# Attention's first batch ends in three steps, its first expert weights arrive earlier

## The chip, the cores and the metric

The kernel runs on one core of a Trainium2 chip. The metric is the device time of one execution, in microseconds (us). TensorE is PE in the profile, VectorE is DVE, ScalarE is ACT, GpSimd is POOL; SyncE (SP) issues every DMA of this kernel, in order.

## The reference

Three parts, each feeding the next.

```
scores = scale * q @ k^T            # 2 batches, 8 heads, 576 positions, head width 64, float32
scores = where(mask, scores, -1e9)  # heads 0-3: the last 32 positions; heads 4-7: every 32nd position
attn   = softmax(scores);  x = attn @ v                 # x: 1152 tokens x 512
p      = domain_probs / sum(domain_probs)               # 4 experts
x      = sum_e p[:, e] * (relu(x @ w1[e]) @ w2[e])      # w1: 512 x 1024, w2: 1024 x 512
out    = (sigmoid(x @ w_gate) * (x @ w_val)) @ w_out    # 512 x 1536, 1536 x 512
```

## The kernel before, in words

Attention comes first, batch by batch. One batch is 16 groups: 8 "s" groups (strided heads 4 to 7, in residues of 8 positions) and 8 "l" groups (local heads 0 to 3). Groups 0 to 15 belong to batch 0, groups 16 to 31 to batch 1. A group passes through stages, one per step of the generator `attention`: scores (PE, two groups at a time, output `sps`), exp (DVE takes the negated row maximum `nm`, ACT the exponentials `P` with their sums `sm`), norm one step later (DVE reciprocal of `sm`, POOL scales `P`), transpose three steps later (PE to `tps`, DVE copies it to `PT`), values (PE to a PSUM tile `o`, for every second group) and split. The split writes x as two parts, `xh` rounded and `xl` the remainder, into tiles of 384 tokens (T = 0, 1, 2): batch 0 fills tile 0 and half of tile 1. For a local group of the second half this is 96 tokens of tile 0 and 192 of tile 1.

The products are made from such pairs: `split_products` issues three matmuls per product (high by high, low by high, high by low). The weights come as float32 `raw` tiles of 512 KB each; `prep_early` turns one into `wh` (an ACT cast) and `wl` (a POOL subtraction), two `early_step` calls for each of its 128-row blocks. Three raw tiles fit at once. `early_up` (four blocks fb of 12 matmuls) and `early_down` are the first expert's units; ACT evacuates an `early_up` block to `hh`, DVE its remainder to `hl`, and DVE evacuates an `early_down` block into `x2acc`, multiplied by `p` (tile `p00`), the token weights. These are computed on DVE from `ptok` (`token_weights`), transposed on PE (`pps`), copied to `ptokT`, written to DRAM (`pd`) and read back spread over all partitions (`p`) by `spread_token_weights`.

The order of the work is the order in which the program is written out: every engine takes its instructions in that order. `attend()` emits one step of attention and, by the step's number, some loads. The first `FIRST_GROUPS` steps are emitted alone (with `early_step` calls between); from then on a step is emitted after every 1 / 0.36 products of the early units. `EMPTY` gives the steps in which PE gets matmuls on zeros (`warm`). `head_start(fb)` issues the first half of block fb of the first `early_up` (the weight rows 2 and 3, which need only the strided heads) ahead of the rest of attention; its PSUM bank stays taken until that block is done.

Eight PSUM banks are in use: the pool `gp` (tag g) has four, `sps` three, the pool `ops` one. All of the transposes, the head starts, the early units' outputs and some `o` tiles take turns in the four banks of `gp`; a new tile waits until all readers of the tile that had the bank before are done. The second strided q and k of batch 1 are in the tile `qk`; `qk_strided` transposes q on PE into `qkps` (ACT copies it to `qsT`), then k (DVE copies it to `ksT`); `qk_local` does the same for the local q and k in three parts.

The three lines on which most depends:

```
gp = ctx.enter_context(tc.tile_pool(name="gp", bufs=PSUM_BUFS, space=PSUM))      # PSUM_BUFS = 4
step_of = [x + DRAIN * (x // (n // B)) for x in range(n)]                        # DRAIN steps between the batches
dve.tensor_tensor(a, ps, pb[e, T], ALU.mult)                                     # early_down's first evacuation, pb is p
```

Of the kernel before, what the change touches and what calls it, by code (L numbers as in the profile page):

```python
# [35 lines left out]
EMPTY = {0: 2, 1: 4, 2: 2, 3: 2, 4: 2, **{i: 2 for i in range(5, 16, 2)}, 16: 1, 19: 1, 20: 1}  # L36
# [11 lines left out]
FIRST_GROUPS = 21  # L48
PT_BUFS = 5
WEIGHTS_FROM = 12  # L50
DRAIN = 5
HEAD_START = (17, 18)
# [54 lines left out]
def attn_moe_glu_kernel(ctx, tc, q, k, v, dp, w1, w2, wg, wv, wo, out):  # L107
# [12 lines left out]
    NU = S // 8  # L120
# [641 lines left out]
    def group_values(g):  # L762
# [20 lines left out]
        if at_step[0] in range(WEIGHTS_FROM, FIRST_GROUPS):  # L783
            of_tiles[g] = o, o
            return
# [4 lines left out]
    def group_split(g):  # L790

        kind, b, c, half, hh = g
        if hh == 0:
            return
        o, of = of_tiles.pop(g)
        low = dve if of is o else pool_
        if kind == "s":
            kk = 2 + c
            hv, ov = (t[:, :288].rearrange("p (a u) -> p a u", u=NU) for t in (o, of))
            for T, off, s0, n in x_parts(b, 0, S):  # L800
                u0, u1 = s0 // 8, (s0 + n) // 8
                sel = lambda t: t[T][:, kk, off:off + n].rearrange("p (u a z) -> p z a u", a=4, z=2)[:, half]
                dve.tensor_copy(sel(xh), hv[:, :, u0:u1])
                low.tensor_tensor(sel(xl), ov[:, :, u0:u1], sel(xh).bitcast(F32), ALU.subtract)
        else:
            for T, off, s0, n in x_parts(b, 288 * half, 288 * half + 288):
                p0 = s0 - 288 * half
                dh, dl = xh[T][:, c, off:off + n], xl[T][:, c, off:off + n]
                dve.tensor_copy(dh, o[:, p0:p0 + n])
                low.tensor_tensor(dl, of[:, p0:p0 + n], dh.bitcast(F32), ALU.subtract)  # L810
# [3 lines left out]
    def attention():  # L814
# [13 lines left out]
        at_stage = {}  # L828
        for name, behind in STAGES:
            for x in range(n):  # L830
                if name in ("values", "split"):
                    if x % QUAD >= 2:
                        at_stage[name, step_of[x] + behind + later(x)] = gs[x]
                elif name == "scores":
                    if x % 2 == 0:
                        at_stage[name, step_of[x]] = gs[x:x + 2]
                else:
                    at_stage[name, step_of[x] + behind] = gs[x]
        qk_strided(0, 0, (0,))
        for i in range(step_of[-1] + STAGES[-1][1] + 1):  # L840
            at_step[0] = i
            for name, _ in STAGES:
                if (name, i) in at_stage:
                    stage[name](at_stage[name, i])
            if i == 0:
                qk_strided(0, 0, (1,))
            if i in HEAD_START:
                head_start(HEAD_START.index(i))
            if i in EMPTY:
                keep_warm(EMPTY[i])  # L850
            for b in range(B):
                at = i - step_of[b * n // B]
                if b and at in (-5, -3):
                    qk_strided(b, 0, (int(at == -3),))
# [388 lines left out]
    with tc.manual_schedule():  # L1243
# [3 lines left out]
        make_constants()  # L1247
        load_local(0)
# [7 lines left out]
        def attend():  # L1256
# [23 lines left out]
        for i in range(FIRST_GROUPS):  # L1280
            attend()
            for _ in range((i >= WEIGHTS_FROM) + (i > 15)):
                early_step(0)
        n_none, n_step = 0, [0]
# [22 lines left out]
        for n, u in enumerate(units):  # L1307
# [33 lines left out]
            for y in unit_steps(u):  # L1341
                if n < N_EARLY:
                    if y is None:
# [45 lines left out]
```

## Time and profile before

| | us |
|---|---|
| median of 3 runs (650.66 to 651.46) | 650.7 |
| the profiled execution | 651.06 |
| its span, first to last instruction | 648.9 |
| PE busy in the span | 638.2 (98%) |
| DVE, ACT, POOL busy | 440.3, 341.7, 265.5 |

The span is 2.2 us shorter than the execution's own time, which also has what lies before the first and after the last instruction. PE's granted clock is full in all 40 slices of the page. A row of the timeline gives the start in the span, the length, the engine, the line in the kernel, the operation with output and inputs, and in brackets how long the engine had been idle and what ended that. Matmul rows overlap, since matmuls are pipelined, so the distance between two starts is what one costs. One transpose, score or value product of float32 can show as two matmuls. Some matmul rows can be missing.

### The profile page before, as it was taken

Reading aid. Unit: us, or ns where it says so; the run is one execution under the profiler, and the core shown is the slowest. Engines: PE = TensorE matmul, PEld = TensorE weight load, DVE = VectorE, ACT = ScalarE, POOL = GpSimd, SP = SyncE. Lnnn points to the kernel's source line nnn. Section 1 sums busy time; section 2 is a strip of 40 time slices with the busy share of each in tenths; the row PEclk is TensorE's granted clock in tenths of the full one; section 3 lists DMA queues with packets and bytes.
Section 4 is the critical chain, followed back from the end, with each engine's and each line's share of the span. In section 5 each row is a group of like instructions: output and inputs, shape, how many; then the busy total and the mean of one; then the engine's idle time right before and its main releaser. Section 6 shows DMA issues by size and latency. Waiting matters only on the chain.

```text
span 648.9 us, 12702 instructions
## 1 busy us (share of the span) xinstructions
PE 638.2 (98%) x4899; PEld 469.3 (72%) x4904; DVE 440.3 (68%) x885; ACT 341.7 (53%) x807; POOL 265.5 (41%) x307
## 2 busy tenths in 40 slices
PE   8889999999999999999999999999999999999998
PEld 5668889999676666666666666666979877987794
DVE  4876586787461886693887788898866659633432
ACT  5747553554854646774645554642565574532230
POOL 3665561000422226361335335440465377453540
PEclk9999999999999999999999999999999999999999
DMA  9965141030421544251664464354113832330002
GB/s 184 243 172 141 35 117 43 1 115 17 142 86 57 158 147 159 81 182 59 183 255 143 163 227 147 98 162 146 35 34 117 286 142 81 107 132 1 33 19 97
DMA packets 48884, 77.00 MB, mean 119 GB/s; under 512 B 19540, under 2 KB 24440, under 8 KB 47672
## 3 DMA queue, kind: packets, MB, share of 16 engines
q1 hardware_dynamic: 48824, 76.20, 37.6%
q8 instruction: 38, 0.62, 0.4%
q14 instruction: 22, 0.18, 0.1%
HBM read 59.66 MB, written 16.53 MB: 117 GB/s over the span
## 4 chain that ended last, share of the span: by engine, by line
PE 94%; DVE 1%; DMA 1%; SPq 1%; ACT 1%; issue 0%; POOL 0%; POOLq 0%; ACTq 0%
PE gps L874 23%; PE gps L876 23%; PE gps L875 23%; PE gps L976 19%; SPq L173 1%; PE sps L730 1%; PE warm L264 1%; PE tps L756 1%; PE o L780 1%; DMA ks<-in_k_dram 1%; ACT P L101 1%; DMA kl<-in_k_dram 1%; PE qkps L698 0%; PE qkps L676 0%; PE sps L717 0%; DVE nm L101 0%
## 5 line engine op out<-in xcount | busy, mean ns | idle before, releaser
L101 POOL TENSOR_TENSOR hl<-t,hh 128x384 f16<-128x384 f32 x72 | 76.5, 1065 | 179.2 <-ACT t L101 175.4
L976 PEld LDWEIGHTS <-w 128*128 128x128 f16 x1512 | 125.0, 98 | 1.8
L976 PE MATMUL gps<-x,w 128*128 128x192 f16 x1512 | 126.2, 246 | 0.0
L874 PE MATMUL gps<-x,w 128*128 128x384 f16 x288 | 93.9, 326 | 0.0
L875 PE MATMUL gps<-x,w 128*128 128x384 f16 x288 | 93.9, 326 | 0.0
L876 PE MATMUL gps<-x,w 128*128 128x384 f16 x288 | 93.9, 326 | 0.0
L874 PE MATMUL gps<-hh,w 128*128 128x384 f16 x288 | 93.9, 326 | 0.0
L875 PE MATMUL gps<-hl,w 128*128 128x384 f16 x288 | 93.9, 326 | 0.0
L876 PE MATMUL gps<-hh,w 128*128 128x384 f16 x288 | 93.9, 326 | 0.0
L874 PEld LDWEIGHTS <-w 128*128 128x128 f16 x576 | 56.4, 98 | 37.3 <-issue 0.2
L876 PEld LDWEIGHTS <-w 128*128 128x128 f16 x576 | 56.4, 98 | 37.2
L875 PEld LDWEIGHTS <-w 128*128 128x128 f16 x576 | 56.4, 98 | 36.4
L101 ACT ACTIVATE hh<-gps 128x384 f16<-128x384 f32 (+1 forms) x96 | 46.8, 487 | 48.8 <-PE gps L876 48.5
L101 POOL TENSOR_TENSOR stage<-magn,stage 128x512 f16<-128x512 f32 x36 | 45.5, 1273 | 45.1 <-ACT magn L101 38.9
L101 ACT ACTIVATE w<-raw,up 128x512 f16<-128x512 f32 x48 | 32.0, 715 | 34.8 <-DVE up L101 34.7
L101 ACT ACTIVATE P<-sps,nm 72x72 f32<-72x72 f32 (+1 forms) x112 | 36.4, 333 | 23.8 <-DVE sm L101 17.0
L101 ACT ACTIVATE bits<-raw 128x512 f32<-128x512 f32 x36 | 24.3, 674 | 38.1 <-DVE magn L101 37.9
L101 DVE SCALAR_TENSOR_TENSOR w<-raw,up,w 128x512 f16<-128x512 f32 x48 | 40.1, 871 | 5.1 <-ACT w L101 4.9
L101 POOL TENSOR_TENSOR sg<-four,sg 128x384 f32<-128x384 f32 x9 | 9.6, 1069 | 80.8 <-DVE four L101 77.9
L874 PE MATMUL gps<-w,hh 128*128 128x512 f16 (+1 forms) x112 | 41.6, 371 | 0.0
L875 PE MATMUL gps<-w,hh 128*128 128x512 f16 (+1 forms) x112 | 41.6, 371 | 0.0
L876 PE MATMUL gps<-w,hl 128*128 128x512 f16 (+1 forms) x112 | 41.6, 371 | 0.0
(145 smaller groups left out, 1281.5 us busy)
## 6 DMA issues: line engine op xcount, KB each, us to landing
raw<-in_moe_w_dram SPq DMA_DIRECT2D x32, 512.0 KB
raw<-in_moe_w_gate_dram SPq DMA_DIRECT2D x12, 512.0 KB
raw<-in_moe_w_val_dram SPq DMA_DIRECT2D x12, 512.0 KB
raw<-in_moe_w_out_dram SPq DMA_DIRECT2D x12, 512.0 KB
wg<-stage SPq DMA_DIRECT2D x21, 256.0 KB
wv<-stage SPq DMA_DIRECT2D x21, 256.0 KB
w<-wg SPq DMA_DIRECT2D x3, 1024.0 KB
wo<-stage SPq DMA_DIRECT2D x12, 256.0 KB
```

The costliest lines, as they stand in the source:

```text
L101: return f(*a, **k)
L173: nc.sync.dma_start(t[:, :, j, :], src[b, 2 * j:2 * j + 2].rearrange("h s d -> (h s) d").rearrange("(c p) d -> p c d", p=128),)
L264: nc.tensor.matmul(ps, zero.to_broadcast([128, 128]), zero.to_broadcast([128, 512]), start=True, stop=True,)
L730: nc.tensor.matmul(pv_[:, j, :], qs_, ks_, start=False, stop=j == m - 1)
L756: nc.tensor.transpose(pv_[:, j, :], pp[:, j, :], ident[:n, :n])
L780: nc.tensor.matmul(o[x * 64:x * 64 + 64, j * n:(j + 1) * n], lhsT, tts[x][:, j, :], start=True, stop=True)
L874: nc.tensor.matmul(ps, ah, bh, start=first and i == 0, stop=False)
L875: nc.tensor.matmul(ps, ah, bl, start=False, stop=False)
L876: nc.tensor.matmul(ps, al, bh, start=False, stop=last and i == n - 1)
L976: nc.tensor.matmul(o, l_, r_, start=first and x + kk + y == 0, stop=last and x * kk * y == 2, skip_group_check=True)
```

## The change

It does six things together.

- The last steps of batch 0 shrink from five (16 to 20) to three (16 to 18): eight entries of the stage table are moved. The values and split of group 11 go from step 17 to 16, the transposes of 14 and 15 from 17 and 18 to 16 and 17, the values of 14 and 15 from 19 and 20 to 18, and these two are split together, tile 0 first. `DRAIN` is 3 and `FIRST_GROUPS` 19.
- `o` alternates between two places: the tile of the second of each pair (`half` for s, `c` for l) comes from `gp`, that of the first from `ops`. In the steps up to 17 ACT copies `o` to `of` and POOL makes `xl`; only in step 18 DVE makes both.
- Three head starts instead of two: blocks 0 and 1 in step 17, block 2 in step 18.
- The first raw tile is loaded ahead of the local q and k of batch 0. `early_step` runs once in each of the steps 4 to 7 and twice in 16 to 18 (before: once in 12 to 15, twice in 16 to 20); in the early units it runs after 0.6 of the products (before 0.5).
- The token weights move from step 18 to 20 and their spreading from 19 to 22, so into the early units; the local v of batch 1 is loaded at step 18.
- The local q and k are transposed in steps 7, 8 and 9 of a batch (before 6, 7 and 9); one matmul on zeros fewer.

```diff
-EMPTY = {0: 2, 1: 4, 2: 2, 3: 2, 4: 2, **{i: 2 for i in range(5, 16, 2)}, 16: 1, 19: 1, 20: 1}
+EMPTY = {0: 2, 1: 4, 2: 2, 3: 2, 4: 2, **{i: 2 for i in range(5, 17, 2)}, 16: 2}
-FIRST_GROUPS = 21
+FIRST_GROUPS = 19
-WEIGHTS_FROM = 12
-DRAIN = 5
-HEAD_START = (17, 18)
+EARLY_STEPS = {4: 1, 5: 1, 6: 1, 7: 1, 16: 2, 17: 2, 18: 2}
+EARLY_RATE = 0.6
+DRAIN = 3
+HEAD_START = {17: (0, 1), 18: (2,)}
...
-        if half and (kind, c) == ("l", 1):
+        if (half if kind == "s" else c):
             o = gp.tile([128, 512], F32, tag="g", name="o")
...
-        if at_step[0] in range(WEIGHTS_FROM, FIRST_GROUPS):
+        if at_step[0] == FIRST_GROUPS - 1:
             of_tiles[g] = o, o
             return
...
-    def group_split(g):
+    def group_split(*gs):
...
+        tiles = [of_tiles.pop(g) for g in gs]
+        for T, off, s0, n in parts:
+            for g, (o, of) in zip(gs, tiles):
+                low = dve if of is o else pool_
...
+                dve.tensor_copy(sel(xh), src(o))
+                low.tensor_tensor(sel(xl), src(of), sel(xh).bitcast(F32), ALU.subtract)
...
+        for name, x, i in (("values", m - 5, m), ("split", m - 5, m), ("transpose", m - 2, m), ("transpose", m - 1, m + 1),
+                           ("values", m - 2, m + 2), ("values", m - 1, m + 2), ("split", m - 2, m + 2), ("split", m - 1, m + 2)):
+            at_stage = {k_: g for k_, g in at_stage.items() if k_[0] != name or g != gs[x]}
+            moved.append((name, i, gs[x]))
...
-            if i in HEAD_START:
-                head_start(HEAD_START.index(i))
+            for fb in HEAD_START.get(i, ()):
+                head_start(fb)
...
-                if at in (6, 7, 9):
-                    qk_local(b, (6, 7, 9).index(at))
+                if at in (7, 8, 9):
+                    qk_local(b, at - 7)
...
         make_constants()
+        load_raw_to(1)
         load_local(0)
...
+            if i == 20:
+                token_weights()
+            if i == 22:
+                spread_token_weights()
             if i == 18:
-                token_weights()
-            if i == 19:
-                spread_token_weights()
-            if i == 20:
                 load_vl(1)
...
-                        n_step[0] += 1
-                        if n_step[0] % 2:
+                        n_step += EARLY_RATE
+                        while n_step >= 1:
                             early_step(n)
+                            n_step -= 1
```

Three places show how the instructions move. On PE, at the end of batch 0: before, the values of 14 and 15 stand apart, and the token weights' transpose `pps` between them.

```order
L676 MATMUL qkps<-ident,qs 128x72 x4
L676 MATMUL qkps<-ident,ks 128x72 x4
L780 MATMUL o<-PT,vl 64x96 x6
L264 LDWEIGHTS const-float32-0.0
L264 MATMUL warm<-const-float32-0.0 128x512
L298 MATMUL pps<-ident,ptok 36x128
L780 MATMUL o<-PT,vl 64x96 x6
L264 LDWEIGHTS const-float32-0.0
L264 MATMUL warm<-const-float32-0.0 128x512
L874 MATMUL gps<-xh_171,wh 128x384
```

And after the change, where the block between values and `qkps` is the third head start, and what follows `qkps` is the rest of block 0:

```order
L781 MATMUL o<-PT,vl 64x96 x12
L889 MATMUL gps<-xh_173,wh 128x384
L890 MATMUL gps<-xl_174,wh 128x384
L891 MATMUL gps<-xh_173,wl 128x384
L889 MATMUL gps<-xh_173,wh 128x384
L890 MATMUL gps<-xl_174,wh 128x384
L891 MATMUL gps<-xh_173,wl 128x384
L677 MATMUL qkps<-ident,qs 128x72 x4
L677 MATMUL qkps<-ident,ks 128x72 x4
L889 MATMUL gps<-xh_173,wh 128x384
```

The transposes of the strided q and k have moved from ahead of the values of 14 and 15 to behind them and behind the third head start. On SP, the first expert's loads and the two DMAs of the token weights; before:

```order
L240 DMA raw<-in_moe_w_dram 128x2x512 x2
L302 DMA pd<-ptokT 36x128
L311 DMA p_101<-pd 128x3x128
L181 DMA vl<-in_v_dram 128x4x64
L185 DMA vl<-in_v_dram 128x5x64 x4
```

After the change:

```order
L182 DMA vl<-in_v_dram 128x4x64
L186 DMA vl<-in_v_dram 128x5x64 x4
L241 DMA raw<-in_moe_w_dram 128x2x512 x3
L303 DMA pd<-ptokT 36x128
L312 DMA p_101<-pd 128x3x128
```

The write `pd` and the read `p` now stand behind the local v of batch 1 and behind three more raw tiles, the last of which waits for a raw buffer. On PE, in the early units after the change, the first use of `hh` is the first `early_down` block, of four products:

```order
L757 MATMUL tps<-ident,P 72x72 x4
L677 MATMUL qkps<-ident,qk_417 128x72 x8
L299 MATMUL pps<-ident,ptok 36x128
L889 MATMUL gps<-hh,wh 128x384
L890 MATMUL gps<-hl,wh 128x384
L891 MATMUL gps<-hh,wl 128x384
L889 MATMUL gps<-hh,wh 128x384
L890 MATMUL gps<-hl,wh 128x384
L891 MATMUL gps<-hh,wl 128x384
L757 MATMUL tps<-ident,P 72x72 x4
```

The transpose `pps`, with which the way of the token weights to `p` begins, stands in the middle of the block whose evacuation is the first to need `p`.

## Rows read from the trace of the kernel before

**Rows 1.** Busy time by stretch: PE, PEld, DVE, ACT, POOL, granted clock, DMA share, GB/s.

```profile
30.00:45.00 15.00, 11.37 (x115) 8.64 (x115) 13.22 (x40) 8.43 (x32) 12.57 (x13) 1.00 0.84 200
45.00:75.00 30.00, 28.84 (x272) 25.34 (x270) 17.97 (x54) 19.45 (x93) 13.79 (x17) 1.00 0.39 105
...
100.00:640.00 540.00, 540.00 (x3963) 391.73 (x3962) 369.58 (x681) 282.04 (x534) 209.11 (x227) 1.00 0.34 114
```

**Rows 2.** PE, 38 to 45 us: start, length, line, operation, [idle before <- releaser].

```profile
38.85 0.47 PE L756 MATMUL tps<-ident,P 96*128 96x96 f32 x3 [0.42 <-POOL P L101]
...
43.15 0.27 PE L298 MATMUL pps<-ident,ptok 128*36 128x128 f32 x1 [1.26 <-DVE ptok L101]
43.34 0.72 PE L780 MATMUL o<-PT,vl 128*64 128x96 f32 x12
44.36 0.38 PE L264 MATMUL warm<-const-float32-0.0 128*128 128x512 bf16 x1 [0.29 <-DVE ptokT L101]
...
44.74 0.34 PE L875 MATMUL gps<-xl,wh 128*128 128x384 f32 x1
```

**Rows 3.** POOL, 35 to 39 us: the scalings of P, groups 14 and 15.

```profile
35.51 0.82 POOL L101 TENSOR_TENSOR P<-P,sm 96x384 f32<-96x384 f32 x1 [0.61 <-ACT wh L101]
...
37.97 0.82 POOL L101 TENSOR_TENSOR P<-P,sm 96x384 f32<-96x384 f32 x1 [0.40 <-DMA kl<-in_k_dram]
```

**Rows 4.** DVE, 42 to 45 us: the split of group 14 into xh and xl.

```profile
42.92 0.24 DVE L101 CAST xh<-o 128x96 fp32r<-128x96 f32 x1
43.20 0.26 DVE L101 TENSOR_TENSOR xl<-o,xh 128x96 fp32r<-128x96 f32 x1
43.38 0.35 DVE L101 CAST xh<-o 128x192 fp32r<-128x192 f32 x1
43.76 0.36 DVE L101 TENSOR_TENSOR xl<-o,xh 128x192 fp32r<-128x192 f32 x1
```

**Rows 5.** DVE, 57 to 60 us: hl, a copy PT, the first use of p.

```profile
57.83 0.56 DVE L101 SCALAR_TENSOR_TENSOR hl<-gps,hh 128x384 fp32r<-128x384 f32 x1 [1.90 <-ACT hh L101]
58.30 0.44 DVE L101 COPY PT<-tps 72x288 f32<-72x288 f32 x1
...
59.40 0.56 DVE L101 TENSOR_TENSOR x2acc<-gps,p 128x384 f32<-128x384 f32 x1
```

**Rows 6.** ACT, 53 to 58 us: exps, the copy qsT, the evacuation hh.

```profile
53.80 0.32 ACT L101 ACTIVATE P<-sps,nm 72x72 f32<-72x72 f32 x1 [1.05 <-DVE sm L101]
...
54.99 0.40 ACT L101 ACTIVATE qsT<-qkps 128x288 f32<-128x288 f32 x1
...
57.28 0.51 ACT L101 ACTIVATE hh<-gps 128x384 fp32r<-128x384 f32 x1
```

**Rows 7.** PE, 54 to 56 us: second transposes of qk, then the first early_down product.

```profile
54.38 0.83 PE L676 MATMUL qkps<-ident,qk 72*128 72x72 f32 x8 [0.35 <-DVE ksT L101]
55.45 0.44 PE L874 MATMUL gps<-hh,wh 128*128 128x384 f32 x1 [0.24 <-ACT qsT L101]
```

**Rows 8.** SP's queue, 44 to 46 us: issue and its length.

```profile
44.33 0.33 SPq L302 DMA_DIRECT2D pd<-ptokT  x1
45.70 0.37 SPq L311 DMA_DIRECT2D p<-pd  x1
```

**Rows 9.** Busy time by stretch again, for its last column, GB/s.

```profile
2.00:6.00 4.00, 4.00 (x18) 1.83 (x17) 0.00 (x0) 0.15 (x2) 2.12 (x6) 1.00 0.68 200
6.00:14.00 8.00, 7.55 (x98) 5.35 (x97) 4.97 (x17) 5.95 (x36) 1.99 (x3) 1.00 1.17 209
...
47.00:48.00 1.00, 1.00 (x13) 0.93 (x10) 0.45 (x1) 0.19 (x1) 0.00 (x0) 1.00 0.52 133
48.00:49.00 1.00, 1.00 (x7) 1.00 (x6) 0.00 (x0) 1.00 (x8) 0.00 (x0) 1.00 0.87 204
```

**Rows 10.** PE, 16 to 19 us: local q transposes of step 6, values of step 7.

```profile
16.91 0.55 PE L698 MATMUL qkps<-ident,ql 128*128 128x128 f32 x3
...
17.71 0.72 PE L780 MATMUL o<-PT,vs 72*64 72x72 f32 x16
```

More of the change, by code (lines that the diff above doesn't have):

```diff
@@ L788, in group_values @@
         of_tiles[g] = o, of
-    def group_split(g):
-        kind, b, c, half, hh = g
-        if hh == 0:
+    def group_split(*gs):
+        for kind, b, c, half, hh in gs:
+            break
+        else:
             return
-        o, of = of_tiles.pop(g)
-        low = dve if of is o else pool_
         if kind == "s":
[L798 to L804, printed above, removed]
-        else:
[L806 to L810, printed above, removed]
+            parts = x_parts(b, 0, S)
+        else:
+            parts = x_parts(b, 288 * half, 288 * half + 288)
+        tiles = [of_tiles.pop(g) for g in gs]
+        for T, off, s0, n in parts:
+            for g, (o, of) in zip(gs, tiles):
+                low = dve if of is o else pool_
+                if kind == "s":
+                    kk, u0, u1 = 2 + g[2], s0 // 8, (s0 + n) // 8
+                    sel = lambda t: t[T][:, kk, off:off + n].rearrange("p (u a z) -> p z a u", a=4, z=2)[:, half]
+                    src = lambda t: t[:, :288].rearrange("p (a u) -> p a u", u=NU)[:, :, u0:u1]
+                else:
+                    p0 = s0 - 288 * half
+                    sel = lambda t: t[T][:, g[2], off:off + n]
+                    src = lambda t: t[:, p0:p0 + n]
+                dve.tensor_copy(sel(xh), src(o))
+                low.tensor_tensor(sel(xl), src(of), sel(xh).bitcast(F32), ALU.subtract)
     at_step = [0]
@@ L844, in attention @@
                     stage[name](at_stage[name, i])
+                both = [g for name_, i_, g in moved if (name_, i_) == (name, i)]
+                if name == "split":
+                    group_split(*both)
+                else:
+                    for g in both:
+                        stage[name](g)
             if i == 0:
                 qk_strided(0, 0, (1,))
-            if i in HEAD_START:
-                head_start(HEAD_START.index(i))
+            for fb in HEAD_START.get(i, ()):
+                head_start(fb)
             if i in EMPTY:
@@ L852, in attention @@
                 at = i - step_of[b * n // B]
-                if b and at in (-5, -3):
-                    qk_strided(b, 0, (int(at == -3),))
+                if b and at in (-3, -1):
+                    qk_strided(b, 0, (int(at == -1),))
                 if at in (2, 3):
                     qk_strided(b, 1, (at - 2,))
-                if at in (6, 7, 9):
-                    qk_local(b, (6, 7, 9).index(at))
+                if at in (7, 8, 9):
+                    qk_local(b, at - 7)
             yield i
@@ L1281, in attn_moe_glu_kernel @@
             attend()
-            for _ in range((i >= WEIGHTS_FROM) + (i > 15)):
+            for _ in range(EARLY_STEPS.get(i, 0)):
                 early_step(0)
-        n_none, n_step = 0, [0]
+        n_none, n_step = 0, 0
         halves = job(x_half())
```

3 lines of the change are left out of this document (2 added, 1 removed).

## The prediction

> **What bounds the kernel now.** I read the busy time by stretch first [rows 1]. From 100 to 640 us PE is busy all 540 us: nothing that this change touches can shorten that, and its instructions there stay in their order. What is open is PE's idle time before: 3.6 us of the 15 from 30 to 45 us, 1.2 of the 30 after that. So the time is PE's work, plus the gaps of the first 75 us.
>
> PE's timeline of the end of batch 0 says what the gaps wait for [rows 2]: POOL's last scaling of P ahead of the transposes of group 15 (0.42 us, at 38.85), the token weights (1.26 us, ahead of `pps` at 43.15), and their copy (0.29 us, at 44.36). The row at 44.74 is the second matmul of the early unit; one lasts 0.18 us from start to start (the distances in the same timeline), so the unit begins at 44.56. I call this moment E. The scaling of group 15 has started at 37.97, 2.5 us after that of group 14 [rows 3].
>
> **The change part by part.** I follow PE from the last common point, and compare moments at which the same work is left.
>
> *Three steps.* The chain to the transposes of 15 is scaling 14, transposes 14, copy PT, reciprocal of `sm` 15 (now behind that copy on DVE), scaling 15. In the profile scaling 14 ends at 36.33 [rows 3]. DVE no longer makes `xl` there, which spares it 0.26 to 0.36 us a time [rows 4]; I let it end at 36.15. Then 0.5 to the start of the copy, 0.44 for it [rows 5], 0.35 for the two small DVE operations (estimate from their distance to the next row), 0.3 to POOL and 0.82 for the scaling: 38.55, against 38.79 before. So the three steps are emitted together but still run one behind the other; PE gains 0.25 us there, and waits in the meantime in place of working. From 38.55 PE has the transposes (0.25), two head starts of 6 matmuls (2.15), the values of both groups (0.7 each by [rows 2]) and the third head start (1.07): 43.4.
>
> *The bank.* Now both strided transposes of batch 1 come. The four banks of `gp` hold three head starts and the `o` of group 15, so the transposes of q wait for the split of 15 on DVE, and those of k for ACT's copy of q: four serial pieces where before there was a spare bank. By the starts at 42.92, 43.38 and (the last row's end) about 44.0, DVE needs 0.46 for the 96 tokens and about 0.65 for the 192 [rows 4]; of the two groups' eight operations two lie beside the values of 15, six follow: 0.2 + 0.46 + 2 x 0.65 = 1.96 after 42.3, so 44.3. PE has waited 0.9. Transposes of q 0.25, ACT's copy with both hand-overs 0.55, transposes of k 0.25: the early unit goes on at 45.3. E is 0.75 later. The two token waits (1.55 us) and a matmul on zeros have gone, the bank's two waits (1.45) and the head start have come.
>
> *What the third head start is worth.* It takes 6 matmuls, 1.07 us, from the early unit. But from E on the attention of batch 1 runs as a chain over ACT that starts with scores 1.6 us after E and is written in the same order as before: `qsT` starts at 54.99 [rows 6], ends at 55.39, 10.83 us after E. PE needs the bank that this copy frees, and goes on at 55.45 [rows 7]. With E at 45.3 that is 56.13, whatever PE has done in between. There PE has two products of `early_down` more behind it than before (1.07 us), and the second transposes of `qk` (0.52) and `pps` (0.2) still ahead: 0.68 later, 0.35 richer, so 0.33 lost. Bounds: -0.7, if DVE's split is as short as the matmuls beside it, to +1.1.
>
> *`pps` waits.* It takes the bank of an earlier transpose, whose copy PT stands on DVE behind `hl`, which needs ACT's `hh` behind `qsT`: 0.4 + 0.56 + 0.44 [rows 5, 6], 1.4 us after `qsT`, while PE has 0.5 us of work. I take 0.8; 0 if another bank is free, 1.2 if the raw cast comes first.
>
> *`p` comes late.* Before, `pd` is issued at 44.33, `p` at 45.70 [rows 8], and the rows by stretch show the 192 KB move mostly from 47 to 49 us [rows 9]; its first use is at 59.40 [rows 5], so it was covered by 10 us. Now the first use stands 1.1 us of matmuls behind `pps`, and DVE, which takes its list in order, stops there: behind it are the copies PT, and PE can go on for about 5.8 us (24 matmuls of 0.18, two sets of transposes of 0.25 and one pair's scores of 1.0, all by the distances between starts) until the transposes that need a bank from behind this point. The path from `pps`: 1.1 to the end of `ptokT` (four DVE operations stand before it), 0.3 to issue, 1.37 to `p`'s issue, 2.3 to 3.3 for `p`, 0.56 for `x2acc`: 5.6 to 6.6, a wait of 0 to 0.8. But `pd` stands on SP behind a raw tile that waits for the last `wl` of the second matrix, at nearly the same time. Its 512 KB at 204 to 209 GB/s [rows 9] are 2.5 us, and all, a part or nothing of that can lie ahead of `pd`. Bounds 0 to 3.3; I take 1.3, with half of it ahead.
>
> The Trainium skill, page "DMA: Bandwidth & Descriptors", section "Queues, rings and completion order", says that each DMA engine takes the descriptors of one ring in ring order. By it the raw tile's data go first in full, and the wait would be 2.3 to 3.3 us in place of 1.3, the sum 1.5 us more. No row here has a small transfer issued right behind a large one, so the trace doesn't decide.
>
> *Raw ahead of local q and k.* 0.52 MB more stand ahead of the strided v of batch 0. From 2 to 14 us the core moves 200 to 209 GB/s [rows 9], so v comes up to 2.5 us later. By bytes (1.18 MB of strided q and k, 1.18 of local, 0.29 of v) it is there at about 14.8 before, 17.3 after. Its first use is at 17.71 [rows 10]; without the local transposes of step 6 (16.91) PE arrives at 17.0. A wait of 0.3, with the landing perhaps 0.8; the scores of groups 8 and 9 and all behind them move by it. I take 0.4, bounds 0 to 1. The casts in steps 4 to 7 fit ACT's and POOL's gaps there, as the `xl` that POOL takes over fits where its `wl` stood; I cost them at nothing, and up to 0.3 if a scaling of P comes behind a `wl`.
>
> Sum: 0.33 + 0.8 + 1.3 + 0.4 = 2.8 us. On the profiled execution's 651.06 this is 653.9; the median of the runs is 0.36 lower, so **653.5**.
>
> **The rivals.** *The waits go and nothing follows (faster).* If the transposes of q find a bank without waiting for the split, E is at 43.9; the chain over ACT then ends 0.7 earlier with 0.35 more done, 1.05 saved, and with `p` in time and `pps` in its place the whole is 0.4 to 1.5 us below: about 649.6. For it speaks that 1.55 us of PE's idle time have one plain cause, which is gone; against it that three head starts leave one bank of four, which is in the code and not a matter of timing.
>
> *No change.* The tail loses 0.3, `pps` some tenths, and `p` is read in 2.3 us with its write ahead of the raw tile: 0.3 + 0.4 + 0.1 = 0.8, or 651.5. For it: DVE is idle for 1.9 us before `hl` at 57.83 [rows 5], so it has room to catch up; against it that SP's order has the raw tile first.
>
> *`p` in full.* If the last `wl` is late as well (its cast stands behind `hh` on ACT), the raw tile, `pd` and `p` all slip behind it: 1 us more on `wl`, 2.8 on `p`, so 0.33 + 0.8 + 1 + 2.8 + 0.4 = 5.3, or 656.0. It decides once the path from `pps` exceeds PE's 5.8 us by more than two.
>
> **How the numbers follow.** The forecast has a chance of 0.45, with its own range 652.2 to 655; `p` in full 0.15, no change 0.25, faster 0.15. The range 649.8 to 656.4 takes in the larger part of the faster case and leaves about 0.1 below and 0.05 above. A difference under 0.2% (1.3 us) can't be told from none, so the borders are 649.4 and 652.0: faster 0.13, same 0.28, slower 0.59 (all but a little of the forecast's and of the last rival's share).
>
> **What would show it.** Right: an idle time of PE near 0.9 us ahead of `qkps` behind the third head start, ended by DVE's `xl`; a second one ended by ACT's `qsT`; the row of `pps` waiting for DVE; a DVE row `x2acc` that waits some microseconds for the DMA of `p`, and a PE idle time of 1 to 3 us at transposes soon after; the values of step 7 waiting for v. Wrong: the early unit's first matmul at or before 44.5, or a first `x2acc` without wait, would take away more than half of the sum.

## The result, and the profile after

The changed kernel takes 659.6 us (median; 659.26 to 661.35) beside 650.75 for the kernel before: ratio 1.0139, interval 1.012 to 1.0158, so 9 us slower. The prediction was 653.5, with a range up to 656.4.

I read the rows by stretch first, as in [rows 1]; the columns are the same, the third number from the right is TensorE's granted clock.

```profile
30.00:45.00 15.00, 12.44 (x119) 9.83 (x120) 8.81 (x30) 8.01 (x36) 11.01 (x14) 0.89 0.74 172
41.00:44.00 3.00, 3.00 (x12) 3.00 (x11) 0.46 (x1) 0.03 (x1) 2.88 (x3) 0.50 0.31 96
45.00:75.00 30.00, 25.16 (x233) 21.80 (x230) 15.62 (x46) 15.63 (x71) 12.34 (x13) 0.94 0.38 105
61.50:64.50 3.00, 2.86 (x13) 2.72 (x14) 2.09 (x7) 2.18 (x11) 2.52 (x3) 0.50 0.18 29
100.00:640.00 540.00, 540.00 (x3992) 395.28 (x3991) 372.85 (x696) 283.14 (x542) 210.30 (x227) 1.00 0.35 114
```

From 100 to 640 us PE is busy all the time, as before. From 45 to 75 us it now idles 4.8 us (1.2 before), and twice, from 41 and from 61 us, the granted clock is 0.50: TensorE at 1.2 in place of 2.4 GHz.

Where the time goes is read at the same points of attention. Rows of PE's timeline of the kernel before that the groups of rows ahead of the prediction do not hold (the first scores, the first local scores, transposes of group 11, of group 19, scores of group 24):

```profile
6.73 0.74 PE L730 MATMUL sps<-ksT,qsT 64*72 64x72 f32 x16 [0.40 <-DVE ksT L101]
20.40 0.90 PE L730 MATMUL sps<-klT,qlT 64*96 64x128 f32 x12
31.07 0.47 PE L756 MATMUL tps<-ident,P 96*128 96x96 f32 x3 [0.63 <-POOL P L101]
61.45 0.42 PE L756 MATMUL tps<-ident,P 72*72 72x72 f32 x4
69.14 0.90 PE L730 MATMUL sps<-klT,qlT 64*96 64x128 f32 x12
```

And PE's timeline of the changed kernel:

```profile
7.23 0.74 PE L731 MATMUL sps<-ksT,qsT 64*72 64x72 f32 x16 [0.27 <-DVE ksT L102]
18.19 0.72 PE L781 MATMUL o<-PT,vs 72*64 72x72 f32 x16 [0.72 <-DMA vs<-in_v_dram]
21.99 0.90 PE L731 MATMUL sps<-klT,qlT 64*96 64x128 f32 x12 [1.03 <-ACT qlT L102]
33.44 0.47 PE L757 MATMUL tps<-ident,P 96*128 96x96 f32 x3 [0.83 <-POOL P L102]
38.40 0.47 PE L757 MATMUL tps<-ident,P 96*128 96x96 f32 x3 [0.82 <-POOL P L102]
40.69 0.63 PE L757 MATMUL tps<-ident,P 96*128 96x96 f32 x3 [0.86 <-POOL P L102]
48.04 0.44 PE L677 MATMUL qkps<-ident,qs 72*128 72x72 f32 x4 [0.81 <-DVE xl L102]
48.98 0.47 PE L677 MATMUL qkps<-ident,ks 72*128 72x72 f32 x4 [0.50 <-ACT qsT L102]
49.26 0.42 PE L889 MATMUL gps<-xh,wh 128*128 128x384 f32 x1
58.62 0.45 PE L889 MATMUL gps<-hh,wh 128*128 128x384 f32 x1 [1.12 <-DVE hl L102]
60.67 0.47 PE L677 MATMUL qkps<-ident,qk 72*128 72x72 f32 x4 [0.47 <-ACT qsT L102]
61.64 0.74 PE L677 MATMUL qkps<-ident,qk 72*128 72x72 f32 x4 [0.50 <-DVE hl L102]
70.94 0.41 PE L757 MATMUL tps<-ident,P 72*72 72x72 f32 x4 [1.43 <-DVE x2acc L102]
78.00 0.90 PE L731 MATMUL sps<-klT,qlT 64*96 64x128 f32 x12 [0.61 <-DVE klT L102]
```

| point of work | before | after | later by |
|---|---|---|---|
| first scores of batch 0 | 6.73 | 7.23 | 0.50 |
| values of step 7 [rows 10] | 17.71 | 18.19 | 0.48 |
| first local scores, step 8 | 20.40 | 21.99 | 1.59 |
| transposes, group 11 | 31.07 | 33.44 | 2.37 |
| transposes, group 15 [rows 2] | 38.85 | 40.69 | 1.84 |
| E, the early unit's first matmul | 44.56 | 49.26 | 4.70 |
| PE goes on behind batch 1's first copy `qsT` of `qk` [rows 7] | 55.45 | 60.67 | 5.22 |
| transposes, group 19 | 61.45 | 70.94 | 9.49 |
| scores, group 24 | 69.14 | 78.00 | 8.86 |
| end of the span | 648.9 | 657.7 | 8.8 |

Nearly all of it is lost by 78 us. The points are not quite the same work: from E on the changed kernel has the six matmuls of its third head start, about 1.05 us, more behind it, and at group 24's scores a third of the local transposes less.

The first 0.50 us can't be laid to the change. Over the profiled executions of this case the first scores start anywhere from 6.03 to 7.23 us, and kernels whose edits all come later stand at both ends. So 1.87 us are lost from there to group 11, where the prediction had put 0.4. Half of the 8.8 is lost by E, the rest while the token weights and `p` are made. DVE and SP show that last part:

```profile
55.88 0.16 DVE L102 TENSOR_REDUCE psums<-ptok 128x9 f32<-128x36 f32 x1
...
56.53 1.56 DVE L102 TENSOR_TENSOR ptok<-ptok,psums 128x36 f32<-128x36 f32 x1
58.02 0.55 DVE L102 SCALAR_TENSOR_TENSOR hl<-gps,hh 128x384 fp32r<-128x384 f32 x1
...
70.23 0.56 DVE L102 TENSOR_TENSOR x2acc<-gps,p 128x384 f32<-128x384 f32 x1 [3.61 <-DMA p<-pd]
```

```profile
62.88 0.37 SPq L241 DMA_DIRECT2D raw<-in_moe_w_dram  x1
63.65 0.34 SPq L303 DMA_DIRECT2D pd<-ptokT  x1
66.83 0.37 SPq L312 DMA_DIRECT2D p<-pd  x1
```

The four token operations take DVE 2.1 us (55.88 to 58.02), `hl` comes behind them, and PE waits 1.12 us for `hl`. `pd` is issued 0.77 us behind a raw tile and takes 3.18 us until `p` can be issued, where it took 1.37 [rows 8]; DVE waits 3.61 us at the first `x2acc`.

### The profile page after: what moved, and what is told of

The parts are those of the page before. It is cut to its first block, busy times and chain, and to the rows that moved or that the text cites. A ratio compares the mean times of both kernels' runs of the same rounds, so it can differ in the third digit from the quotient of the medians.

```text
span 657.7 us, 12705 instructions
## 1 busy us (share of the span) xinstructions
PE 642.1 (98%) x4897; PEld 471.9 (72%) x4903; DVE 436.2 (66%) x881; ACT 342.7 (52%) x810; POOL 268.5 (41%) x311
## 4 chain that ended last, share of the span: by engine, by line
PE 90%; DVE 3%; ACT 2%; DMA 2%; SPq 2%; issue 1%; POOL 1%; POOLq 0%; DVEq 0%
PE gps L889 23%; PE gps L890 22%; PE gps L891 22%; PE gps L991 19%; ACT P L102 1%; SPq L174 1%; PE o L781 1%; PE sps L731 1%; DMA vs<-in_v_dram 1%; PE tps L757 1%; DVE nm L102 1%; DVE sm L102 1%; DMA p<-pd 1%; DMA pd<-ptokT 0%; POOL P L102 0%
```

## The experiments

All were timed beside the kernel before. Each ratio is to it, with its interval; where a gain or loss is given in us without more, it is worked out from the ratios. Executions of one kernel differ by whether and where the granted clock falls in them. The kernel before shows a mean clock of 0.999 or 1.0 in 66 of its 69 executions beside the other kernels (650.87 us on average) and 0.997 in three (652.49 to 652.66).

### Parts of the change taken back

**Token weights early.**

```diff
-            if i == 20:
+            if i == 17:
                 token_weights()
-            if i == 22:
+            if i == 18:
                 spread_token_weights()
```

> Token weights computed at step 17 and spread at step 18 (in the changed kernel they come at 20 and 22, inside the early unit). Theory A, the token work is in the way twice: its four DVE operations (2.1 us by the trace of the changed kernel) stand ahead of hl, for which TensorE waits 1.12 us, and p lands after its first use, for which DVE waits 3.61 and TensorE 1.43. Both waits go, and if the second fall of the granted clock (62 to 65 us) follows from them, it goes as well (12 matmuls at 0.32 in place of 0.18 us, 1.7 us); pps now waits about 0.5 us for DVE's ksT. 659.6 - 1.1 - 1.4 - 1.7 + 0.5 = 655.9. Rival B, the chain over ACT sets the pace of batch 1 and the waits only slide to qsT and klT: 658.5 or more. Rival C, the granted clock falls again in this stretch whatever waits there are: about 657.6.

657.15 us, 1.0094 (1.008 to 1.0108): about 2.9 us of the 9. The waits went nearly as theory A says: none at `x2acc`, 0.55 at `pps`, but for `hl` 0.55 is left of the 1.12. And 655.9 is missed: the granted clock fell all the same (0.50 from 61 to 64 us), and PE waited 1.10 for `xl` in place of 0.81, since the token operations now stand on DVE ahead of the split, one of them very long:

```profile
41.88 2.12 DVE L102 TENSOR_SCALAR psums<-psums 128x9 f32<-128x9 f32 x1
```

Rival C is nearest.

**Local transposes back.**

```diff
-                if at in (7, 8, 9):
-                    qk_local(b, at - 7)
+                if at in (6, 7, 9):
+                    qk_local(b, (6, 7, 9).index(at))
```

> Local transposes of q and k back at steps 6, 7 and 9 of each batch (7, 8 and 9 in the changed kernel), all else as changed. Theory A: at step 7 the copy qlT stands on ACT behind four exponentials of the same step, and the first local scores of step 8 wait 1.03 us for it; with the transposes a step earlier that wait goes, and the wait of 0.72 us for vs is partly filled by them (0.6 us of transposes): 659.6 - 1.0 - 0.6 = 658.0. The same in batch 1, where klT is waited for 0.61 us: at most 0.4 more, 657.6. Rival D: scaling of P on POOL is the chain of these steps and the scores wait anyway: 659.3.

657.91, 1.0095 (1.0079 to 1.0112): the median lies where A expected it, 1.7 us below 659.6; by the ratios it is 2.9 us less. The wait for `qlT` ahead of the scores of step 8 is gone, that for `vs` too; one of 0.78 ahead of a transpose, for `sm`, is new. The profiled execution (655.92) has no stretch at the lower clock, which makes it the clean look at the bank:

```profile
39.63 0.47 PE L757 MATMUL tps<-ident,P 96*128 96x96 f32 x3 [0.85 <-POOL P L102]
...
45.42 0.44 PE L677 MATMUL qkps<-ident,qs 72*128 72x72 f32 x4 [0.81 <-DVE xl L102]
46.36 0.47 PE L677 MATMUL qkps<-ident,ks 72*128 72x72 f32 x4 [0.50 <-ACT qsT L102]
46.64 0.42 PE L889 MATMUL gps<-xh,wh 128*128 128x384 f32 x1
```

From the transposes of group 15 to E it takes 7.01 us; the prediction had 45.3 - 38.55 = 6.75. In the changed kernel it is 8.57: the first fall of the clock costs 1.56 there. Not every fall costs as much in the end: another execution of this kernel has a mean clock of 0.996 and takes 656.01.

**Raw tile late again.**

```diff
-EARLY_STEPS = {4: 1, 5: 1, 6: 1, 7: 1, 16: 2, 17: 2, 18: 2}
+EARLY_STEPS = {12: 1, 13: 1, 14: 1, 15: 1, 16: 2, 17: 2, 18: 2}
...
-        load_raw_to(1)
         load_local(0)
```

> First raw tile loaded behind local q and k and strided and local v again, and its four preparation steps at steps 12 to 15 (4 to 7 in the changed kernel). Theory A: the wait of 0.72 us for vs goes, and with the casts out of steps 6 and 7 the scaling of P and the exponentials behind them come 0.4 to 0.5 us earlier; but the same casts and wl stand in steps 12 to 15 ahead of scalings of P, where the kernel before had waits of 0.4 to 0.7 us. Net 0 to 1.2 us: 658.4 to 659.6. Rival E, the early raw tile is the main cause of the 2.4 us that step 11 is late: 657.2.

661.32, 1.0157 (1.0143 to 1.0171): not better, by the ratios 1.2 us worse, though the intervals touch. Both theory A, which expected up to 1.2 us less, and rival E fall. The wait for `vs` is gone, but the last scaling of P comes later, and the clock is at 0.50 from 39 to 45.5 us and from 73 to 76.4:

```profile
40.67 0.74 PE L757 MATMUL tps<-ident,P 96*128 96x96 f32 x3 [1.41 <-POOL P L102]
```

**Token weights and local transposes together** (both edits above).

> The changed kernel with both edits that gave time alone: token weights at steps 17 and 18, local transposes at steps 6, 7 and 9. Theory A, they are separate waits, and the gains (2.9 us each by the ratios) add up: 653.9; in a run without a fall of the granted clock 653. Rival B, one chain hides the other's waits: 655.5. What is left against the kernel before is then the three steps, the bank waits and the raw tile ahead.

655.56, 1.0075 (1.0061 to 1.0089). The gains overlap: 4.2 us in place of 5.8. It lies at rival B's 655.5; every execution still shows a fall (here 59.5 to 62.5 us).

**The same with two head starts.**

```diff
-HEAD_START = {17: (0, 1), 18: (2,)}
+HEAD_START = {17: (0, 1)}
```

> The same with two head starts in place of three, so that a bank of gp is free when the strided transposes of batch 1 come. Theory G, the bank: the waits ahead of the transposes of q (0.81 to 1.10 us in the runs so far), of k (0.50) and of pps (0.55) go or shrink, and the third head start's six matmuls come back in the early unit, where they fill waits for ACT: 0.5 to 1.5 us below the kernel with three, 652.4 to 653.4. Rival H, the third head start is worth its 1.07 us and the transposes wait for ACT's and DVE's copies anyway: the same as with three or 0.5 above.

654.46, 1.0052 (1.004 to 1.0064): 1.5 us below the kernel with three, by the ratios, whose intervals just touch. The transposes of q no longer wait, though `pps` behind them now waits 0.89 for the split. The difference is the one that theory G expected; the third head start costs more than its matmuls bring. Three of the six executions have a mean clock of 0.999 or 1.0 and take 653.74 to 654.06: some 3 us above the kernel before are lost without any fall to speak of.

**Two head starts in the changed kernel itself**: the last edit alone.

> The changed kernel with two head starts in place of three, nothing else (token weights at 20 and 22, local transposes at 7, 8 and 9). Theory G, the bank: the wait for xl ahead of the transposes of q (0.81 us) goes; 1.0 to 2.0 us less than the changed kernel, as with the token weights and local transposes moved (1.5 us): 657.6 to 658.6. Rival H, the third head start is worth what the bank's wait costs: 659.3 or more.

657.98, 1.0111 (1.0098 to 1.0124): 1.8 us less, in G's range, though the intervals overlap by a little. The wait for `vs` is 1.81 us in this execution (0.72 in the changed kernel), so `vs` lands at quite different times.

### Parts of the change alone

**The raw part on the kernel before.**

```diff
+        load_raw_to(1)
         load_local(0)
...
-            for _ in range((i >= WEIGHTS_FROM) + (i > 15)):
+            for _ in range((4 <= i < 8) + 2 * (i > 15)):
                 early_step(0)
```

> The kernel before with the raw part of the change alone: first raw tile loaded ahead of local q and k, its four preparation steps at 4 to 7 in place of 12 to 15 (local transposes at 6, 7, 9, remainder, banks and token weights as before). Theory A: vs is late (it was waited for 0.72 us in the changed kernel, but here 0.7 us of local transposes stand ahead of it), 0 to 0.3 us lost; wl no longer stands ahead of the scalings of P at 31 to 36 us, where TensorE waits 0.63 and 0.72: 0.3 to 0.9 gained. 650.0 to 651.0. Rival E, the early raw tile costs what it cost in the changed kernel's first 22 us: 652 or more.

651.94, 1.0022 (1.0012 to 1.0032): 1.4 us lost, at rival E's edge. PE waits 0.36 for `vs`, and 0.61 and 0.71 for scalings of P as before, so what A hoped to gain is not there. A wait for a scaling is new:

```profile
24.09 0.44 PE L756 MATMUL tps<-ident,P 72*72 72x72 f32 x4 [0.75 <-POOL P L101]
```

That scaling (from 23.37 on POOL) stands behind a `wl` that runs from 21.70 to 22.97, one of the two that have moved to the steps 4 to 7. From the first scores to the transposes of group 11 it takes 25.55 us, 24.34 before.

**The late local transposes on the kernel before.**

```diff
-                if at in (6, 7, 9):
-                    qk_local(b, (6, 7, 9).index(at))
+                if at in (7, 8, 9):
+                    qk_local(b, at - 7)
```

> The kernel before with one part of the change: local transposes at steps 7, 8 and 9 of each batch in place of 6, 7 and 9. Theory A: the copy qlT of step 7 stands behind four exponentials, and the first local scores wait about 1.0 us for it as in the changed kernel, in the same place in both batches (in batch 1 most is hidden by early products): 0.8 to 1.4 us more, 651.6 to 652.2, and a fall of the granted clock in some executions on top. Rival O, the wait was from the early casts of the changed kernel on ACT: 650.8, no change.

652.7, 1.0037 (1.0022 to 1.0051): 2.4 us lost by the ratio, with no other edit. Two of the eight executions have falls of the clock (653.97 and 656.01); the other six are at full clock and take 652.5 on average, 1.6 us above the kernel before. Theory A's range of 0.8 to 1.4 us is passed by a little. The same wait is there, without any early cast:

```profile
21.28 0.90 PE L730 MATMUL sps<-klT,qlT 64*96 64x128 f32 x12 [1.11 <-ACT qlT L101]
```

ACT's row of `qlT` starts at 20.73, behind eight exponentials of two groups and a copy, which run from 18.05 with hardly a gap. Rival O falls. From the first scores to the transposes of group 11 it takes 25.51 us, 1.17 more than before.

**Three steps without the raw part**: the three edits of the kernel at 1.0052 (token weights, local transposes, two head starts) and that of the late raw tile.

> The three steps alone: the changed kernel with two head starts, token weights at steps 17 and 18, local transposes at 6, 7 and 9, and the raw tile loaded and prepared as before (steps 12 to 15). Beside the kernel with the same edits and the raw tile ahead (1.0052 of before). Theory J, the casts of steps 12 to 15 stand on POOL ahead of the scalings of groups 14 and 15, which three steps put closer together, so the wait ahead of the last transposes grows to 1.4 us, and the granted clock falls there: 655.5 or more. Rival K, the raw part costs 1.4 us here as it does in the kernel before: 652.7.

655.64, 1.0072 (1.0059 to 1.0085), as theory J expected. Beside 1.0052 with the raw tile ahead, and 1.0022 for the raw part alone: the three steps (with all that goes with them, moved token weights and two head starts) cost 0.72% alone, and in their company the early raw tile is worth 0.2% in place of costing it, though the two intervals touch. The wait ahead of the last transposes is 1.52 us, as J has it, and J's reason is half of the story. POOL and DVE:

```profile
35.67 0.82 POOL L102 TENSOR_TENSOR P<-P,sm 96x384 f32<-96x384 f32 x1 [0.40 <-DVE sm L102]
...
37.21 1.26 POOL L102 TENSOR_TENSOR wl<-raw,wh 128x512 fp32r<-128x512 f32 x1
38.87 0.82 POOL L102 TENSOR_TENSOR P<-P,sm 96x384 f32<-96x384 f32 x1 [0.40 <-DVE sm L102]
```

```profile
37.43 1.07 DVE L102 TENSOR_SCALAR sm<-sm 96x3 f32<-96x3 f32 x1
38.53 0.17 DVE L102 RECIPROCAL sm<-sm 96x3 f32<-96x3 f32 x1
```

The scaling queues behind `wl`, which ends at 38.47, and then waits 0.40 us more for its `sm`: DVE's addition to it, 3 columns wide, takes 1.07 us while `wl` runs and ends with it (0.15 to 0.17 otherwise). Scaling 15 starts 3.20 us behind scaling 14, 2.28 in the changed kernel. Had the addition taken 0.15, POOL would still have been in `wl` until 38.47, so of these 0.9 us some 0.5 are the queue and 0.4 the addition.

### The granted clock

**Zeros in the waits around group 14's transposes.**

```diff
-EMPTY = {..., 16: 2}
+EMPTY = {..., 16: 5}
...
                     for g in both:
+                        if (name, i) == ("transpose", m):
+                            keep_warm(3)
                         stage[name](g)
```

> Three matmuls on zeros ahead of the transposes of group 14 and three more behind them, about 0.64 us each time, in waits that the changed kernel has there (0.82 and 0.86 us). Theory F, the first fall of the granted clock (41 to 44.6 us) follows from these waits: with them filled the clock stays at 1.0, and the 12 products of the head starts and the values cost 1.7 us less: 657.9. If the fall is from what lies before 37 us, or the zeros do not count, the time stays at 659.6; if the zeros push the transposes, up to 660.2. By rival C (the falls cost nothing in the end, since ACT's chain sets the pace) the clock stays up and the time is still 659.3 or more.

659.22, 1.0124 (1.011 to 1.0138): by the ratio 1 us less, but the intervals overlap, and theory F's 657.9 is missed. The clock holds from 30 to 45 us, and falls elsewhere, behind a wait of 1.39 us for `vs`:

```profile
19.00:21.00 2.00, 2.00 (x10) 1.53 (x11) 1.32 (x6) 0.81 (x4) 0.08 (x1) 0.50 1.24 211
30.00:45.00 15.00, 13.85 (x146) 10.07 (x147) 9.71 (x34) 8.45 (x38) 11.11 (x15) 1.00 0.74 163
```

**Zeros in four waits**: the same, and two more steps.

```diff
-EMPTY = {..., 16: 5}
+EMPTY = {..., 6: 3, 16: 5, 18: 3}
```

> The changed kernel with matmuls on zeros in four of its waits: three at step 6 (ahead of the wait for vs), three ahead of and three behind the transposes of group 14, three at step 18 (ahead of the transposes of q that wait for the split), 0.64 us each time. Theory F: the granted clock falls where TensorE has waited much, in another place from run to run; with the waits of 17 to 48 us filled, only falls behind 55 us are left: 1.7 us less than the changed kernel by the price of one fall, 658.0, and mean granted clocks of 0.997 and above. Rival C, the falls come by themselves or cost nothing: 659.5, clocks 0.992 to 0.997 as before.

659.68, 1.0148 (1.0128 to 1.0169): nothing gained. The stretch to 45 us keeps its clock, and behind the waits of 57 to 60 us it falls for 10 us:

```profile
45.00:59.00 14.00, 11.30 (x94) 9.35 (x95) 6.61 (x18) 7.30 (x33) 4.33 (x5) 1.00 0.47 114
60.00:69.00 9.00, 8.87 (x47) 8.02 (x48) 3.38 (x12) 3.98 (x19) 5.11 (x5) 0.50 0.29 83
```

Theory F's first half holds (filled waits, no fall there), its price does not: the fall moved. Nor is the clock the whole loss: one execution has a mean clock of 0.999 and still takes 659.19.

**No zeros in the kernel before** from step 5 on.

```diff
-EMPTY = {0: 2, 1: 4, 2: 2, 3: 2, 4: 2, **{i: 2 for i in range(5, 16, 2)}, 16: 1, 19: 1, 20: 1}
+EMPTY = {0: 2, 1: 4, 2: 2, 3: 2, 4: 2}
```

> The kernel before without its matmuls on zeros from step 5 to 20 (15 of them, 0.21 us each, most in waits of TensorE), all else as before. Theory F: the granted clock now falls in the stretch of 15 to 45 us as it does in the changed kernel, once or twice, 1.7 us each time, while the waits themselves stay: 652.5 to 654.2, mean clock 0.992 to 0.997. Rival C, the clock holds: 650.3 to 650.9, since the zeros lie in waits.

651.95, 1.0007 (0.9997 to 1.0017). Ten of its eleven executions have a mean granted clock of 0.995 to 0.997 and take 651.22 to 652.01; the one at 1.0 takes 649.86. So taking the zeros away does make the clock fall here, where it fell in three of 69 executions with them, and a fall costs some 2 us (one execution on the other side); the three executions of the kernel before give 1.7. Rows of one with the fall:

```profile
38.00:40.00 2.00, 2.00 (x9) 1.91 (x9) 1.58 (x5) 0.00 (x1) 1.78 (x2) 0.50 0.82 202
```

By that one execution the zeros cost a little themselves, about 1 us, which the expectation (652.5 to 654.2) had not allowed for.

### Where the token work stands in the kernel before

**Spread behind the values of 15.**

```diff
-            if i == 19:
-                spread_token_weights()
             if i == 20:
+                spread_token_weights()
                 load_vl(1)
```

> The kernel before with one edit: the token weights are spread at step 20 in place of 19, so that pps stands behind the values of group 15 and not ahead of them. Theory A, the order alone makes TensorE wait 1.26 and 0.29 us there: ptok is ready at 43.0, the values of 15 fill the time, 0.7 to 1.5 us gained: 649.4 to 650.2. Rival B, the path over DVE's split and ACT sets when batch 1 starts: 650.9 as now.

650.7, 0.9996 (0.9987 to 1.0004): no clear change, and at most 0.85 us gained, though the wait of 1.26 us at `pps` shrank to 0.30 and the one for `ptokT` went. PE and DVE:

```profile
43.41 0.27 PE L298 MATMUL pps<-ident,ptok 128*36 128x128 f32 x1 [0.30 <-DVE ptok L101]
43.48 0.44 PE L874 MATMUL gps<-xh,wh 128*128 128x384 f32 x1
...
44.60 0.44 PE L874 MATMUL gps<-xh,wh 128*128 128x384 f32 x1 [0.20 <-DVE xh L101]
```

```profile
42.25 1.01 DVE L101 TENSOR_TENSOR ptok<-ptok,psums 128x36 f32<-128x36 f32 x1
...
44.29 0.25 DVE L101 CAST xh<-o 128x96 fp32r<-128x96 f32 x1
```

PE starts the early unit a microsecond sooner (43.48, where E was 44.56) and needs 1.12 us for its first three products in place of 0.55, since it stops for `xh` of group 15, which stands on DVE behind the token operations. Rival B holds in the main: most of PE's wait was cover for DVE's queue.

**Token weights a step earlier**, the spread as in the last one.

```diff
-            if i == 18:
+            if i == 17:
                 token_weights()
```

> The kernel before with the token weights computed at step 17 and spread at step 20 (18 and 19 before). With the spread alone moved TensorE's wait of 1.26 us went and the time stayed; the early unit then waited for xh of group 15. Theory L: the split of group 15 on DVE ends the path there, and DVE's four token operations (1.6 to 1.9 us) stand ahead of it; a step earlier they take DVE's idle time of 1.1 us ahead of ksT, the split and E come 0.7 to 1.1 us earlier: 649.6 to 650.1. Rival M, the copy PT of group 15 behind the token operations is as late as the split gets early: 650.7 as now.

652.54, 1.0027 (1.0017 to 1.0036): slower, which neither theory expected. The copy PT behind the token operations frees the bank of the transposes of k late (PE waits 1.56 there), and every execution has a clock of 0.997.

**Token weights behind the split.**

```diff
-            if i == 18:
+            if i == 20:
                 token_weights()
+                load_vl(1)
-            if i == 19:
+            if i == 21:
                 spread_token_weights()
-            if i == 20:
-                load_vl(1)
```

> The kernel before with the token weights computed at step 20, behind the split of group 15, and spread at step 21, in the early unit. Theory L: in the trace with the spread moved alone, the early unit began at 43.48 and stopped until 44.60 for xh of group 15, which stood on DVE behind the token operations (1.6 us); without them ahead the split ends that much earlier, batch 1 begins 0.7 to 1.1 us earlier, and p, first used some 14 us later, is in time: 649.6 to 650.1. Rival B: the path over ACT's copies and exponentials absorbs it: 650.4 to 650.8. Rival N, hl of the first head start now stands behind the token operations: 650.8 to 651.5.

649.36, 0.9974 (0.9965 to 0.9984): faster than both kernels, and by 1.7 us than the kernel before (1.45 by the medians). Theory L holds:

```profile
42.02 0.25 DVE L101 CAST xh<-o 128x96 fp32r<-128x96 f32 x1
...
43.82 0.20 DVE L101 TENSOR_TENSOR ptok<-ptok,psums 128x36 f32<-128x36 f32 x1
```

The split of 15 starts 3.88 us behind the transposes of 15 (38.14 here) in place of 5.38 (44.23 by DVE's timeline of the kernel before), and DVE does the token work where it would have waited for `hh`. That the transposes themselves are 0.71 us earlier here is no gain of the edit: the first scores of this execution are 0.70 earlier (6.03).

## Why the prediction was wrong, step by step

*What bounds the kernel*: right. The sign was right, and the place in the main (waits of PE in the first 75 us, but also ahead of 30 us, where the prediction looked for 0.4); the size was a third.

| stretch | forecast | measured |
|---|---|---|
| to the transposes of group 11 | 0.4 | 2.37, of which 0.50 at the first scores |
| from there to E | 0.74 | 2.33 |
| from E to the end | 1.69 | 4.1 |
| sum | 2.83 | 8.8 |

*Three steps*: right as told. The scaling of 15 starts 2.28 us behind that of 14 (37.53 and 39.81 on POOL) in place of 2.46 [rows 3]; 0.25 was forecast, 0.18 came. From the transposes of group 11 to those of 15 the kernel gains 0.53 us.

*The bank*: right, to a tenth: waits of 0.81 and 0.50 where 0.9 and 0.55 stood. With two head starts the wait for the split ahead of the transposes of q goes, and 1.5 to 1.8 us come back. So *What the third head start is worth* was too kind: 0.33 lost was forecast, its removal gains about 1.5. Its frame held, though: from E until PE goes on behind `qsT` the prediction took 10.89 us (44.56 to 55.45), and it is 10.80 with the token weights early (48.87 to 59.67) and 11.41 in the changed kernel.

*`p` comes late*: the mechanism was right, and the size came near by luck. DVE waits 3.61 and PE 1.43; 1.3 was taken for PE. From `pps` (62.17) to the end of the first `x2acc` (70.79) it takes 8.6 us. The prediction's path of 5.6 to 6.6 with the whole raw tile ahead (2.5) is 8.1 to 9.1, with half of it 6.9 to 7.9. So the whole tile was ahead. `pd` took 1.8 us longer with the tile issued 0.77 us before it, together about the 2.5 that its data need. The rule of the Trainium skill (DMA: Bandwidth & Descriptors, section Queues, rings and completion order), by which the raw tile goes first, is what the runs side with. PE's wait is near the value with half only because PE had 7.3 us of work behind `pps` (62.17 to 69.51) where 5.8 were forecast; its clock had just fallen.

***`pps` waits* failed in part.** `pps` itself waited for nothing. The chain that was described, a bank behind `hl` behind `hh` behind `qsT`, is there one instruction earlier, ahead of the transposes of k at 61.64: 0.50 us where 0.8 stood. What the prediction left out is the token operations' place on DVE. I had counted their time only as delay of `p`; in fact they stand ahead of an earlier `hl`, for which PE waits 1.12 us. The prediction named "four DVE operations" and did not ask who is queued behind them. About half of the wait is theirs: 0.55 stays with the token weights early, and the stretch from E until PE goes on behind `qsT` is 0.6 us longer with them there.

**The baseline of *The bank* misled too**: "The two token waits (1.55 us) ... have gone" was taken as a gain. It changed no term of the sum, since E was followed forward from group 15, but the rival *The waits go and nothing follows* rests on it. With the spread alone moved, most of that wait goes and little or no time comes; with DVE's token work moved behind the split, 1.7 us come. What ended the path there was DVE's queue, more than the wait that PE showed.

***Raw ahead of local q and k* failed in size, and no term of the sum was missed by more**: 0.4 was taken, 1 at most; from the first scores to group 11, 1.87 us are lost. The wait for `vs` was there (0.72, between 0.3 and 1.8 in the runs), but it stands where the local transposes stood, and the values of step 7 come no later behind the first scores than before (10.96 and 10.98 us). Two things were left out. The casts, put at nothing and at most 0.3, make a scaling of P late: PE waits 0.75 for it with the raw part alone, which costs 1.4 us in all. And the move of the local transposes, which I counted only as sparing PE 0.7 us, costs 1.6 us alone at full clock: `qlT` is one step later on ACT, behind eight exponentials, and the scores of step 8 need it at once. Up to group 11 the two cost 1.21 and 1.17 us alone and 1.87 together.

**A term that was missing, the granted clock.** In the profile before it is 1.0 throughout, and I forecast waits without asking what they do to it. In the changed kernel it falls twice; the first costs 1.56 us of E, nearly all that is beyond the forecast from group 15 to E. The second falls while `p` is on its way, so part of it only shortens that wait.

From ratio to ratio, each step down with its edits: 1.0139, token work and local transposes back 1.0075, third head start out 1.0052, three steps (and the banks of `o`, the early rate and the rest that goes with them) undone 1.0022, raw part undone 1. In us 4.2, 1.5, 2.0 and 1.4. The order matters: the parts overlap, and each one's share of the falls of the clock can't be told apart. The 2.0 us of the three steps were not taken further apart, and why `vs` lands at such different times was not settled.

## What to carry to other kernels

A wait that the profile shows on the busiest engine is a gain only if nothing else arrives at the same moment: look at what the next instruction needs, and on which queue it stands. When work is moved to a later step, list what is behind it on its new engine's queue, and when a copy is moved a step later, look who reads it in that same step. The kernel before, with waits of 0.4 to 1.3 us, held the full granted clock in nearly every execution, and the changed one, with a few more such waits, in none of its four (0.992 to 0.997), so waits that are added are to be costed with the clock. And when two profiles are compared, look first whether they start alike: here the first scores alone differ by 1.2 us over the kernels.

## What the runs showed of the hardware

A small DVE operation on SBUF data can last until POOL's operation beside it ends. The multiplication of `ptok`, 36 columns, takes 0.20 us in the last kernel above, where POOL is idle at that moment, and 1.01 and 1.56 us where a `wl` runs beside it:

```profile
56.76 1.28 POOL L102 TENSOR_TENSOR wl<-raw,wh 128x512 fp32r<-128x512 f32 x1
```

This one ends at 58.04, the multiplication at 58.09; it had started at 56.53, while a scaling of P ran on POOL (56.13 to 56.79). The addition to `psums` took 2.12 us in the kernel with the token weights early, 0.17 in the changed one. The addition to `sm`, 0.15 us alone, took 0.3 to 1.3 us in four to seven places of a run's first 90 us; reciprocals and copies from PSUM beside it kept their 0.17 and 0.44. The Trainium skill, page "SBUF — State Buffer", section "SBUF: two separate sides", says that GpSimd and some operations of DVE, those with two inputs in SBUF among them, share a pair of ports that one of the two holds for a whole instruction; the trace agrees for the multiplication, which has two such inputs. With the three steps alone the long addition to `sm` is 0.4 of the 0.9 us by which the scaling of group 15 is late.

The clock fell with no single wait of PE above 0.9 us ahead of it (0.83, 0.82 and 0.86 between 31 us and the fall at 41), and where zeros filled some waits the fall came behind others.
